# Plain outer products for the last item, splits ahead of everything else, and a GpSimd that stops computing earlier

## The chip, the cores and the metric

The kernel runs on one core of a Trainium2 chip. The metric is the device time of one execution in microseconds. TensorE (PE) does the matrix products, VectorE (DVE), ScalarE (ACT) and GpSimd (POOL) the elementwise work, and SyncE (SP) issues the DMAs.

## The reference

Attention with pooled keys and values, followed by a gated pair of matrix products, all in float32:

```
k_p, v_p = mean of k, v over 8 neighbouring positions
attn = softmax(q @ k_p.T / 8);  x = attn @ v_p       8 batches x 8 heads x 576 x 64
x -> 4608 tokens x 512
out = ((x @ w_a) * (x @ w_b)) @ w_out                512 -> 1536 -> 512
```

## The kernel before

**Precision.** Every float32 operand is split into a high part (a cast to fp32r on ACT, written with `nc.scalar.copy`) and a low part (the difference, a `tensor_tensor` subtraction, line 281, on DVE or POOL). A product is then three matmuls: high x high, high x low, low x high (lines 1352 to 1354 for inner products, 1459 to 1461 for outer ones).

**Tiling.** The tokens are taken in 6 pairs of two halves of 384 columns. The hidden width of 1536 is taken in 6 items (`j`) of two 128-row tiles. The first pair is computed with plain products. From the second pair on (`"s"` items, the ones with `p` from 1 to 5) the inner products x @ w_a and x @ w_b are done by a Strassen-like scheme with seven products in place of eight (`PRODUCTS7`). Its right operands B11, B21, T2, T1, T3, B22, T4 are made once for each pair by `prepare`: four combinations (L1099, 768 columns) and seven splits (ACT L1093, DVE or POOL L281), into the tiles `xB..` and `xT..`, of which there is one each, so that a split can run only when the pair before has used that operand for the last time. For pairs `p` from 2 on the outer products too have seven in place of eight (`OUTER7`): the gated products C11, C12, C21, C22 (the tiles `h`) are combined (L1267) and split (ACT L1259, DVE L281) into seven operands `hh` by `operands_of`, and `outer_block` does 7 products for each of 2 column parts, 42 matmuls an item, in two PSUM banks (`accX`, `accY`); after each product of three matmuls DVE adds the bank to the result `y` in SBUF (L1492), which frees it.

**Order.** The order of the work on all engines is written out by a planner in the kernel (`Machine`), which runs at build time: each piece of work has a duration, a rank (lower goes first) and conditions, and each engine takes the lowest rank that is ready. `TOP` is -1000; what empties PSUM has rank TOP or TOP + 1, gated operands TOP + 2, `prepare` a due time, the outer products 1e4 and the inner ones 2e4. The chip then executes these fixed orders with semaphores. `either` (line 271) offers a `tensor_tensor` of SBUF operands to DVE and to POOL, whichever is free first; from item number `ALONE` on, DVE alone gets it. There are 38 items: 8 of the first pair (numbers 0 to 7), then six for each of the other pairs, so number 8 is the first item of the second pair and number 14 the first of the third. In the planner, POOL's work and DVE's work of SBUF operands exclude each other. Beside the items, the attention of the next pair (`chunk`), the sums of weights for the Strassen-like products (`block_sums`) and those for the outer products (`sums_outer`, which stores its splits in DRAM as `kept_outer`) run at lower rank.

Of the kernel before, what the change touches and what calls it, by code (L numbers as in the profile page):

```python
# [9 lines left out]
F32 = mybir.dt.float32  # L10
# [73 lines left out]
SUMS_STEP = 1  # L84
SUMS_RANK = 320.0
SPARE = 1

ALONE = 14

MARGIN = 0.5  # L90

# [152 lines left out]
def attn_moe_kernel(ctx: ExitStack, tc: tile.TileContext, q, k, v, vr, wa, wb, wo, out):  # L244
# [249 lines left out]
    def sums_outer():  # L494

        for j in range(NJ):
            yield until(("kept", "raw o", 2 * j), ("kept", "raw o", 2 * j + 1))
            yield lambda: at_item[0] >= SUMS_FROM + j * SUMS_STEP and slots.can("rawo")() and len(slots.free) > SPARE
            r = slots.take("rawo", j, [P, 2, 512], F32)
            for y in range(2):  # L500
                yield transfer(r[:, y], kept["raw o", 2 * j + y], 1 << 18)
            kept["outer", j] = dr.tile([P, 2, 7, 2, P], F32, name=f"kept_outer_{j}")
            a11, a21, a12, a22 = (r[:, y, x:x + 256] for y in range(2) for x in (0, 256))

            def split(src, n, at):
                yield lambda: slots.can("osum")() and len(slots.free) >= SPARE
                e = slots.take("osum", (j, at), [P, 2, 2, 2, P], F32R)[:, :, :n]
                by = src.rearrange("p (o c s) -> p c o s", o=n, c=2)

                yield on_act(n * 256, lambda: [nc.scalar.copy(e[:, c, :, 0], by[:, c]) for c in range(2)], 2)  # L510
                yield either(n * 256, lambda eng: [low_part(eng, e[:, c, :, 1], by[:, c], e[:, c, :, 0]) for c in range(2)], 2)
                start(1e4, store(e, n, at))

            def store(e, n, at, j=j):
                for c in range(2):
                    dst = kept["outer", j][:, c, at:at + n].rearrange("p o l s -> p (o l s)")
                    yield transfer(dst, e[:, c].rearrange("p o l s -> p (o l s)").bitcast(F32), n << 17)
                mark("kept", "outer", j, at)
                slots.give("osum", (j, at))

            yield from split(r[:, 1], 2, 5)
            yield from split(a11, 1, 0)
            for out_, a, b, how in (
                (a22, a21, a22, ALU.add),
                (a21, a11, a21, ALU.subtract),
                (a11, a22, a11, ALU.subtract),
                (a12, a12, a11, ALU.subtract),
            ):
                yield either(256, lambda eng: eng.tensor_tensor(out=out_, in0=a, in1=b, op=how))
# [553 lines left out]
    def prepare(p):  # L1083
        yield lambda: have(2 * p)() and have(2 * p + 1)()
        t = xraw[p]
        b11, b12, b21, b22 = (t[:, r:r + 2, c:c + HB] for r in (0, 2) for c in (0, HB))
        rank = due_item[items.index(("s", p, 0))] - 20

        def split(name, src, *after):
            x = RIGHT.index(name)  # L1090
            yield until(("used", p - 1, x), *after)
            to = operand(p, name)
            yield on_act(2 * HB, lambda: nc.scalar.copy(to[:, 0], src))  # L1093
            yield low(2 * HB, to[:, 1], src, to[:, 0])
# [12 lines left out]
        start(rank + 2, combine(t2, b22, b11, "T2", ("T1", p)))  # L1107
        start(rank + 3, split("T2", t2, ("T2", p)))
        start(rank + 4, split("T1", b11, ("T2", p)))
        start(rank + 5, combine(b12, b22, b12, "T3", ("T1", p)))  # L1110
        start(rank + 6, split("T3", b12, ("T3", p)))
        start(rank + 7, split("B22", b22, ("T2", p), ("T3", p)))
        start(rank + 8, combine(b21, b21, t2, "T4", ("T2", p), ("operand", p, "B21")))
        start(rank + 9, split("T4", b21, ("T4", p)))
# [39 lines left out]
    def load_outer():  # L1154
        for x, name in enumerate(order_o):
            if name is None:
                continue
            j, c, second = name
            yield until(*(("kept", "outer", j, at) for at in (0, 1, 3, 5)))
            yield lambda: slots.can("wo")() and next_o[0] == x  # L1160
            next_o[0] += 1
            ops = slice(4 * second, 4 + 3 * second)
            e = slots.take("wo", x, [P, ops.stop - ops.start, 2, P], F32R)
# [79 lines left out]
    def hh_count(item):  # L1243
        if item[0] == "n":
            return 2 * len(item[1])
        return 4 if item[1] < 2 else 7

    hh_before = {item: sum(hh_count(x) for x in items[:number]) for number, item in enumerate(items)}

    def operands_of(item):  # L1250
# [150 lines left out]
    def outer():  # L1401

        x = 0
        for item in items:
            kind, p, j = item
            if kind == "s" and p >= 2:
                yield from outer_block(item, x)
                x += 4
# [6 lines left out]
            for half in halves(item):  # L1415
                yield lambda: all((item, 2 * j + y, half) in gs for y in range(2))
                for c in range(DM // P):
# [22 lines left out]
                    start(TOP + 1, taken_outer(p if kind == "s" else 0, half, c, bank, pt, opens, closes))  # L1440

    def outer_block(item, x0):
        _, p, j = item
        for c in range(2):
# [5 lines left out]
            for n, (left, right, bank, opens, what) in enumerate(OUTER7):  # L1450
# [18 lines left out]
                start(TOP + 1, taken_outer(p, half, row, bank, pt, j == 0 and first, j == NJ - 1 and last))  # L1469
            for e in ws:  # L1470
                start(TOP, give_slot(e))

    def give_operand(item, name):
        yield m.SETTLE
# [7 lines left out]
    def taken_outer(p, half, c, bank, pt, opens, closes):  # L1482
# [11 lines left out]
            mark("opened", p, half, c)  # L1494
        if p >= 2:
            yield MARGIN
        acc_free[bank] = True
# [107 lines left out]
```

## Time and profile before

| | |
|---|---|
| median of 3 runs | 1017.22 us (1015.75 to 1017.97) |
| profiled execution | 1016.27 us, span 1014.5 us |
| PE busy | 968.1 us, 95%, 5776 matmuls |
| DVE busy | 855.7 us, 84% |
| ACT busy | 579.5 us, 57% |
| POOL busy | 168.0 us, 17%, the last subtractions near 402 us |
| mean granted TensorE clock | 0.990 |

Times in the rows are microseconds from the start of the span, durations in us in the timeline and in ns where a group's mean is given. PE = matmuls of TensorE. The granted clock is given as a share of full speed. Stage by stage: the first pair ends about 226 us, the second about 398, the third begins there; the last item's inner products end near 998 us.

### The profile page before, as it was taken

To read this page: it belongs to the slowest core of one execution; us is meant where nothing else is said; L and a number is where in the kernel's file an instruction comes from. 1 tells how busy PE (TensorE), PEld (TensorE's weight loads), DVE (VectorE), ACT (ScalarE), POOL (GpSimd) and SP (SyncE) were. 2 spreads that over 40 slices of the span, in tenths; PEclk is the share of its full clock that TensorE was granted. 3 is DMA by queue.
4 is the path that set the end of the run, shared out by engine and by line. 5 is a ranking of instruction groups with operands and counts; after the bars stand their busy time and mean duration, and the time that the engine had idled before them with its cause. 6 is when DMAs were issued, how large, how long until landed. Compare 5 with 4: busy or idle time off the path is not lost.

```text
span 1014.5 us, 17014 instructions
## 1 busy us (share of the span) xinstructions
PE 968.1 (95%) x5776; PEld 953.0 (94%) x5776; DVE 855.7 (84%) x1681; ACT 579.5 (57%) x1584; POOL 168.0 (17%) x162
## 2 busy tenths in 40 slices
PE   4689999999999897999999999999999999999997
PEld 3589999999999897999999899999999999999996
DVE  7988896589897788769898988989989888968777
ACT  4789896647865565465455475455466555342331
POOL 4331233165345445000000000000000000000000
PEclk9989999999999998999999999999999999999999
DMA  9768855568876876868675696866778666796661
GB/s 311 239 229 280 283 183 191 172 206 279 302 258 237 291 278 228 302 224 313 243 272 193 221 334 222 297 234 213 268 260 311 229 224 208 258 322 239 236 208 63
DMA packets 88342, 250.16 MB, mean 247 GB/s; under 512 B 9856, under 2 KB 17536, under 8 KB 88256
## 3 DMA queue, kind: packets, MB, share of 16 engines
q1 hardware_dynamic: 88256, 249.08, 70.5%
q8 instruction: 46, 0.75, 0.3%
q14 instruction: 40, 0.33, 0.1%
HBM read 197.13 MB, written 51.90 MB: 245 GB/s over the span
## 4 chain that ended last, share of the span: by engine, by line
PE 86%; DVE 9%; ACT 2%; issue 1%; DVEq 0%; ACTq 0%
PE acc L1459 6%; PE acc L1461 6%; PE acc L1460 6%; PE psc L913 5%; PE psXB L1352 4%; PE psXB L1353 4%; PE psXB L1354 4%; PE psXA L1354 4%; PE psXA L1352 4%; PE psXA L1353 4%; PE psYA L1352 3%; PE psYA L1353 3%; PE psYA L1354 3%; PE psYB L1352 3%; PE psYB L1354 3%; PE psYB L1353 3%
## 5 line engine op out<-in xcount | busy, mean ns | idle before, releaser
L1492 DVE TENSOR_TENSOR y<-acc,y 128x384 f32<-128x384 f32 x304 | 165.0, 552 | 26.5 <-PE acc L1461 22.0
L1259 ACT CAST hh<-h 128x384 fp32r<-128x384 f32 x168 | 85.3, 516 | 92.0 <-DVE h L1397 45.5
L281 DVE TENSOR_TENSOR hh<-h,hh 128x384 fp32r<-128x384 f32 x210 | 118.1, 580 | 5.7 <-ACT hh L1306 3.3
L1459 PE MATMUL acc<-hh,wo 128*128 128x384 f32 x336 | 116.5, 347 | 1.9 <-DVE y L1492 1.2
L1460 PE MATMUL acc<-hh,wo 128*128 128x384 f32 x336 | 114.0, 339 | 2.1 <-DVE hh L281 2.0
L1461 PE MATMUL acc<-hh,wo 128*128 128x384 f32 x336 | 113.7, 338 | 0.0
L875 ACT ACTIVATE weights<-psc,least 128x72 f32<-128x72 f32 x240 | 73.8, 330 | 38.3 <-DVE least L891 34.2
L1379 ACT COPY h<-psXA 128x384 f32<-128x384 f32 x90 | 43.2, 480 | 78.2 <-PE psXA L1354 77.6
L913 PE MATMUL psc<-kdiag,qh 128*128 128x144 f32 x320 | 59.4, 286 | 11.5 <-ACT kdiag L653 10.4
L1459 PEld LDWEIGHTS acc<-hh,wo 128*128 128x128 f32 x336 | 63.5, 189 | 4.9 <-DVE y L1492 3.3
L1460 PEld LDWEIGHTS acc<-hh,wo 128*128 128x128 f32 x336 | 63.6, 189 | 2.9 <-DVE hh L281 2.9
L913 PEld LDWEIGHTS psc<-kdiag,qh 128*128 128x128 f32 x320 | 54.4, 204 | 12.4 <-issue 8.0
L1461 PEld LDWEIGHTS acc<-hh,wo 128*128 128x128 f32 x336 | 63.5, 189 | 0.0
L1267 DVE TENSOR_TENSOR h<-h,h 128x384 f32<-128x384 f32 x96 | 52.7, 549 | 0.5
L1003 ACT CAST turned<-ptr 128x512 fp32r<-128x512 f32 x72 | 40.4, 593 | 19.9 <-PE ptr L996 19.7
L875 ACT ACTIVATION_READ_ACCUMULATOR weights<-psc,least 128x1 f32 x240 | 51.6, 215 | 0.0
L818 POOL MEMSET qh<- 128x256 f32 x4 | 1.2, 311 | 296.6 <-PE psc L913 296.6
L1397 DVE TENSOR_TENSOR h<-h,h 128x384 f32<-128x384 f32 x85 | 49.5, 582 | 0.5
L1353 PE MATMUL psXA<-xT,load 128*128 128x384 f32 x144 | 48.6, 337 | 0.8 <-DVE xT L281 0.8
L1352 PE MATMUL psXA<-xT,load 128*128 128x384 f32 x144 | 48.9, 339 | 0.0
L1352 PE MATMUL psXB<-xT,load 128*128 128x384 f32 x144 | 48.5, 337 | 0.0
L1353 PE MATMUL psXB<-xT,load 128*128 128x384 f32 x144 | 48.5, 337 | 0.0
(301 smaller groups left out, 3165.4 us busy)
## 6 DMA issues: line engine op xcount, KB each, us to landing
load<-kept_S SPq DMA_DIRECT2D x96, 512.0 KB, 4.8
load<-kept SPq DMA_DIRECT2D x72, 512.0 KB, 5.1
wo<-kept_outer SPq DMA_DIRECT2D x48, 512.0 KB, 4.5
wo<-kept_outer SPq DMA_DIRECT2D x48, 384.0 KB, 3.9
kept_S<-sum SPq DMA_DIRECT2D x24, 512.0 KB, 3.2
kept_outer<-osum SPq DMA_DIRECT2D x36, 256.0 KB, 3.6
out<-y SPq DMA_DIRECT2D x48, 192.0 KB, 2.2
kept<-sum SPq DMA_DIRECT2D x18, 512.0 KB, 6.7
```

The source lines that it names most:

```text
L281: eng.tensor_tensor(out=lo, in0=src, in1=hi.bitcast(F32), op=ALU.subtract)
L875: nc.scalar.activation(s[:n, h], src[:, h - hs.start], AF.Exp, bias=least[:n, h:h + 1], scale=SCALE, accum_out=z[:n, h:h + 1],)
L913: nc.tensor.matmul(pt[:n, j * hk:(j + 1) * hk], qq[:, g, cs], kd[:, g, w].rearrange("p e s -> p (e s)"), start=(x == 0), stop=(x == len(to ...
L1259: yield on_act(HB, lambda: nc.scalar.copy(e[:, 0], gf[item, src]))
L1267: yield either(HB, lambda eng: eng.tensor_tensor(out=t, in0=ta, in1=tb, op=ALU.subtract))
L1352: nc.tensor.matmul(pt, w[:, 0, mat, c], xo[:, 0, kk], start=(opens and kk == 0), stop=False, **more)
L1353: nc.tensor.matmul(pt, w[:, 0, mat, c], xo[:, 1, kk], start=False, stop=False, **more)
L1354: nc.tensor.matmul(pt, w[:, 1, mat, c], xo[:, 0, kk], start=False, stop=(kk == 1), **more)
L1459: nc.tensor.matmul(pt, w[:, 0], e[:, 0], start=opens, stop=False, **more)
L1460: nc.tensor.matmul(pt, w[:, 0], e[:, 1], start=False, stop=False, **more)
L1461: nc.tensor.matmul(pt, w[:, 1], e[:, 0], start=False, stop=True, **more)
L1492: yield on_dve(HB, lambda: nc.vector.tensor_tensor(out=acc[at], in0=pt, in1=acc[at], op=ALU.add))
```

## The change

Three edits. (1) The last item of all does its outer products plainly: eight products (of two terms each for a row and a column half) instead of seven, on the four unmodified gated products, in six PSUM banks (the two accumulators, two banks of the inner products and the two of the attention), where the two terms of a result are added up in the bank. For this the left operand `a21` is split once more in `sums_outer` and stored, and the last item's loads hold 4 operands each. (2) The seven splits of `prepare` get the rank -999.5, just behind what empties PSUM at TOP and ahead of the adds at TOP + 1 and the gated operands at TOP + 2; the combinations keep theirs. (3) `ALONE` becomes 8 in place of 14.

```
+SPLIT_RANK = -999.5
-ALONE = 14
+ALONE = 8
...
-            kept["outer", j] = dr.tile([P, 2, 7, 2, P], F32, name=f"kept_outer_{j}")
+            kept["outer", j] = dr.tile([P, 2, 8, 2, P], F32, name=f"kept_outer_{j}")
...
             yield from split(a11, 1, 0)
+            if j == NJ - 1:
+                yield from split(a21, 1, 7)
...
-        start(rank, split("B11", b11))
+        start(SPLIT_RANK, split("B11", b11))
         start(rank, combine(b11, b12, b11, "T1", ("operand", p, "B11")))
-        start(rank + 1, split("B21", b21))
+        start(SPLIT_RANK, split("B21", b21))
...
         if kind == "s" and item[1] >= 2:
-            order_o += [(j, c, x) for c in range(2) for x in range(2)]
+            order_o += [(j, c, x, 4 if item == items[-1] else 4 - x) for c in range(2) for x in range(2)]
...
         rank = TOP + 2
+        if item == items[-1]:
+            for name, what in (("B11", "C11"), ("B22", "C22"), ("B12", "C12"), ("B21", "C21")):
+                start(rank, split(name, what, what))
+                start(rank, leave(what, "split " + name))
+            return
...
+    def outer_last(item, x0):
+        _, p, j = item
+        ws = {}
+        for c in range(2):
+            for x in range(2):
+                yield lambda: x0 + 2 * c + x in loaded_o
+                ws[c, x] = loaded_o.pop(x0 + 2 * c + x)[2]
+        banks = {}
+        a11, a12, a21, a22 = 0, 5, 7, 6
+        first = [("C11", a11), ("C21", a21)]
+        steps = [(0, *x, "B11", True, False) for x in first]
+        for c in range(2):
+            for what, l1, l2 in (("C12", a11, a12), ("C22", a21, a22)):
+                steps += [(c, what, l1, "B12", True, False), (c, what, l2, "B22", False, True)]
+        steps += [(1, *x, "B11", True, False) for x in first]
+        steps += [(c, what, left, "B21", False, True) for c in range(2) for what, left in (("C11", a12), ("C21", a22))]
+        bank_of = {"C11": ("X", "YA"), "C21": ("Y", "YB")}
+        for c, what, left, right, opens, ends in steps:
+            yield lambda: (item, right) in gq
...
+            def products():
+                nc.tensor.matmul(pt, w[:, 0], e[:, 0], start=opens, stop=False)
+                nc.tensor.matmul(pt, w[:, 0], e[:, 1], start=False, stop=False)
+                nc.tensor.matmul(pt, w[:, 1], e[:, 0], start=False, stop=ends)
+            yield on_pe(mms(3, HB), products, 1e4)
+            if ends:
+                half, row = int(what[2]) - 1, 2 * (int(what[1]) - 1) + c
+                start(TOP + 1, taken_outer(p, half, row, place, pt, False, True))
```

The rest of the diff hands `taken_outer` the bank together with the table in which it is marked free.

## Rows read from the trace of the kernel before

**Rows 1.** The page: busy time of three engines (share of the span, instructions) and the granted clock in 40 slices of 25.4 us.
```profile
PE 968.1 (95%) x5776; PEld 953.0 (94%) x5776; DVE 855.7 (84%) x1681; ACT 579.5 (57%) x1584; POOL 168.0 (17%) x162
POOL 4331233165345445000000000000000000000000
PEclk9989999999999998999999999999999999999999
```

**Rows 2.** Table of stretches: the stretch and its length, then busy us (and instructions) of PE, PEld, DVE, ACT and POOL, the granted clock, the DMA share and GB/s.
```profile
226.00:412.00 186.00, 176.01 (x1045) 172.35 (x1044) 158.81 (x286) 120.86 (x345) 87.16 (x73) 0.97 0.75 264
310.00:340.00 30.00, 26.83 (x152) 25.76 (x151) 20.96 (x39) 16.77 (x51) 14.54 (x14) 0.94 0.70 250
340.00:370.00 30.00, 29.28 (x177) 28.88 (x176) 27.64 (x53) 19.28 (x57) 15.64 (x16) 1.00 0.81 293
398.00:412.00 14.00, 10.27 (x48) 10.23 (x49) 9.67 (x13) 4.68 (x8) 3.85 (x3) 0.76 0.38 131
640.00:740.00 100.00, 100.00 (x595) 99.66 (x594) 94.04 (x196) 51.42 (x142) 0.57 (x2) 1.00 0.73 253
700.00:740.00 40.00, 40.00 (x231) 40.00 (x230) 39.39 (x79) 19.00 (x44) 0.00 (x0) 1.00 0.79 275
```

**Rows 3.** Waits of PE over 226 to 412 us: who waited for whom, us in total, times, the longest.
```profile
PE acc_s L1428 <- DVE hh L281: 5.0, 1, 5.0
PE psXB L1352 <- DVE h L1385: 1.3, 2, 0.7
PE ptr L996 <- ACT pr L970: 1.2, 1, 1.2
PE ptr L996 <- DVE rem L281: 0.9, 1, 0.9
```

**Rows 4.** Timeline at the boundary of the second and third pair: start, duration, engine, line, operation, out<-in, and in brackets the idle time before it and who ended that.
```profile
395.20 2.14 POOL L1099 TENSOR_TENSOR xraw<-xraw 128x768 f32<-128x768 f32 x1
395.58 2.57 DVE L281 TENSOR_TENSOR xT<-xraw,xT 128x768 fp32r<-128x768 f32 x1
397.29 2.52 POOL L1099 TENSOR_TENSOR xraw<-xraw,T 128x768 f32<-128x768 f32 x1
398.07 3.60 DVE L281 TENSOR_TENSOR hh<-h,hh 128x384 fp32r<-128x384 f32 x2
401.73 0.69 PE L1428 MATMUL acc_s<-hh,wo 128*128 128x384 f32 x1 [5.03 <-DVE hh L281]
```

**Rows 5.** Groups of DVE instructions over 226 to 410 us, shapes kept apart: busy us and mean ns of one, then the idle time before them.
```profile
L281 DVE TENSOR_TENSOR hh<-h,hh 128x384 fp32r<-128x384 f32 x23 | 17.5, 766 | 1.4 <-ACT hh L1306 1.0
L1397 DVE TENSOR_TENSOR h<-h,h 128x384 f32<-128x384 f32 x13 | 9.9, 765 | 0.1
L891 DVE TENSOR_SCALAR least<-m 128x4 f32<-128x4 f32 x13 | 6.1, 468 | 0.4
L281 DVE TENSOR_TENSOR xT<-xraw,xT 128x768 fp32r<-128x768 f32 x2 | 3.5, 1758 | 0.0
```

**Rows 6.** The same forms, and one of 512 columns, over 420 to 1000 us.
```profile
L281 DVE TENSOR_TENSOR hh<-h,hh 128x384 fp32r<-128x384 f32 x165 | 87.3, 549 | 1.8 <-ACT hh L1259 1.7
L1397 DVE TENSOR_TENSOR h<-h,h 128x384 f32<-128x384 f32 x71 | 39.0, 549 | 0.4
L281 DVE TENSOR_TENSOR pr<-weights,pr 128x512 fp32r<-128x512 f32 x17 | 11.6, 681 | 0.0
L281 DVE TENSOR_TENSOR xT<-xraw,xT 128x768 fp32r<-128x768 f32 x9 | 8.5, 947 | 0.0
L891 DVE TENSOR_SCALAR least<-m 128x4 f32<-128x4 f32 x32 | 5.4, 170 | 1.1
```

**Rows 7.** Timeline of the end, PE and DVE.
```profile
996.04 0.56 DVE L1397 TENSOR_TENSOR h<-h,h 128x384 f32<-128x384 f32 x1
996.30 0.34 PE L1459 MATMUL acc<-hh,wo 128*128 128x384 f32 x1
997.86 0.37 PE L1459 MATMUL acc<-hh,wo 128*128 128x384 f32 x1
999.68 0.45 PE L1460 MATMUL acc<-hh,wo 128*128 128x384 f32 x1 [1.44 <-DVE hh L281]
1010.86 0.34 PE L1461 MATMUL acc<-hh,wo 128*128 128x384 f32 x1
1011.24 0.56 DVE L1492 TENSOR_TENSOR y<-acc,y 128x384 f32<-128x384 f32 x1 [0.21 <-PE acc L1461]
```

**Rows 8.** The DMA queue of SP in the timeline of the end (the last four loads of outer weights), and two groups of DMA issues of the page (count, size of one, us to landing).
```profile
973.41 8.21 SPq L278 DMA_DIRECT2D wo<-kept_outer  x4
...
wo<-kept_outer SPq DMA_DIRECT2D x48, 512.0 KB, 4.5
out<-y SPq DMA_DIRECT2D x48, 192.0 KB, 2.2
```

**Rows 9.** The costliest group of POOL over 226 to 412 us.
```profile
L281 POOL TENSOR_TENSOR sum<-sums,sum 128x512 fp32r<-128x512 f32 x12 | 16.2, 1348 | 29.3 <-ACT sum L571 25.7 <-PE acc_s L1429 2.7 <-DMA o<-kept_ro 0.9
```

**Rows 10.** Waits of PE over 530 to 575 us, around the boundary of the third and fourth pair.
```profile
PE psXA L1353 <- DVE xT L281: 0.8, 1, 0.8
PE acc L1460 <- DVE hh L281: 0.5, 1, 0.5
```

More of the change, by code (lines that the diff above doesn't have):

```diff
@@ L1103, in prepare @@
         t2 = slots.take("T2", p, [P, 2, HB], F32)
-        start(rank, split("B11", b11))
+        start(SPLIT_RANK, split("B11", b11))
         start(rank, combine(b11, b12, b11, "T1", ("operand", p, "B11")))
-        start(rank + 1, split("B21", b21))
+        start(SPLIT_RANK, split("B21", b21))
         start(rank + 2, combine(t2, b22, b11, "T2", ("T1", p)))
-        start(rank + 3, split("T2", t2, ("T2", p)))
-        start(rank + 4, split("T1", b11, ("T2", p)))
+        start(SPLIT_RANK, split("T2", t2, ("T2", p)))
+        start(SPLIT_RANK, split("T1", b11, ("T2", p)))
         start(rank + 5, combine(b12, b22, b12, "T3", ("T1", p)))
-        start(rank + 6, split("T3", b12, ("T3", p)))
-        start(rank + 7, split("B22", b22, ("T2", p), ("T3", p)))
+        start(SPLIT_RANK, split("T3", b12, ("T3", p)))
+        start(SPLIT_RANK, split("B22", b22, ("T2", p), ("T3", p)))
         start(rank + 8, combine(b21, b21, t2, "T4", ("T2", p), ("operand", p, "B21")))
-        start(rank + 9, split("T4", b21, ("T4", p)))
+        start(SPLIT_RANK, split("T4", b21, ("T4", p)))
         yield until(("operand", p, "T2"), ("T4", p))
@@ L1157, in load_outer @@
                 continue
-            j, c, second = name
+            j, c, second, n = name
             yield until(*(("kept", "outer", j, at) for at in (0, 1, 3, 5)))
+            if second and n == 4:
+                yield until(("kept", "outer", j, 7))
             yield lambda: slots.can("wo")() and next_o[0] == x
             next_o[0] += 1
-            ops = slice(4 * second, 4 + 3 * second)
-            e = slots.take("wo", x, [P, ops.stop - ops.start, 2, P], F32R)
+            ops = slice(4 * second, 4 * second + n)
+            e = slots.take("wo", x, [P, n, 2, P], F32R)
             src = kept["outer", j][:, c, ops].rearrange("p o l s -> p (o l s)")
@@ L1245, in hh_count @@
             return 2 * len(item[1])
-        return 4 if item[1] < 2 else 7
+        return 4 if item[1] < 2 or item == items[-1] else 7
     hh_before = {item: sum(hh_count(x) for x in items[:number]) for number, item in enumerate(items)}
@@ L1405, in outer @@
             kind, p, j = item
+            if item == items[-1]:
+                yield from outer_last(item, x)
+                continue
             if kind == "s" and p >= 2:
@@ L1439, in outer @@
                         opens, closes = j == LEAD, j == LEAD - 1
-                    start(TOP + 1, taken_outer(p if kind == "s" else 0, half, c, bank, pt, opens, closes))
+                    start(TOP + 1, taken_outer(p if kind == "s" else 0, half, c, (acc_free, bank), pt, opens, closes))
     def outer_block(item, x0):
@@ L1468, in outer_block @@
                 last = what not in [t[4] for t in OUTER7[n + 1:]]
-                start(TOP + 1, taken_outer(p, half, row, bank, pt, j == 0 and first, j == NJ - 1 and last))
+                start(TOP + 1, taken_outer(p, half, row, (acc_free, bank), pt, j == 0 and first, j == NJ - 1 and last))
             for e in ws:
                 start(TOP, give_slot(e))
+    def outer_last(item, x0):
[17 more added lines that the diff above has]
+            yield lambda: (item, right) in gq
+            if opens and what in bank_of:
+                name = bank_of[what][c]
+                free = acc_free if name in acc_free else readable
+                yield lambda: free[name]
+                free[name] = False
+                tag = "acc" + name if name in acc_free else name
+                pt = ps.tile([P, HB], F32, tag=tag, name=f"acc_{p}_{j}_{c}_{what}")
+                banks[c, what] = pt, (free, name)
+            elif opens:
+                yield bank_there
+                pt, tag = take_bank(f"acc_{p}_{j}_{c}_{what}")
+                banks[c, what] = pt[:, :HB], tag
+            pt, place = banks[c, what]
+            e, w = gq[item, right][0], ws[c, left // 4][:, left % 4]
+            def products():
[6 more added lines that the diff above has]
+                start(TOP + 1, taken_outer(p, half, row, place, pt, False, True))
@@ L1496, in taken_outer @@
             yield MARGIN
-        acc_free[bank] = True
+        if isinstance(bank, str):
+            give_bank(bank)
+        else:
+            bank[0][bank[1]] = True
         if closes:
```

## The prediction

> **What bounds the kernel now.** I read the page first. TensorE is busy for 95% of the span, VectorE (DVE) for 84%, GpSimd (POOL) for 17%, and all of that POOL time lies in the first 16 of the 40 slices [rows 1]. So the time is TensorE's stream of matmuls plus the places where the stream is broken. Next I looked for those breaks with the table of stretches. Over 640 to 740 us TensorE is busy for all of 100 us although DVE is busy for 94.0 of them, and over 700 to 740 it still loses nothing with DVE at 39.4 of 40; nothing can be won there [rows 2]. In the stage of the second pair, 226 to 412 us (the only steady stage that still has POOL work), TensorE is busy for 176.0 of 186 us, and the granted clock is 0.94 over 310 to 340 and 0.76 over 398 to 412 [rows 2]. At half clock a microsecond does half the work, so the mean says what is lost: 0.06 x 30 = 1.8 us and 0.24 x 14 = 3.4 us, together 5.2. The view of waits gives the rest: the four largest waits of TensorE in that stage sum to 5.0 + 1.3 + 1.2 + 0.9 = 8.4 us [rows 3]. So the stage holds 13.6 us of breaks, and TensorE itself needs 186 - 13.6 = 172.4.
>
> The timeline shows where the 5.0 comes from. At 395.58 a DVE subtraction of 768 columns takes 2.57 us and the two of 384 columns behind it 3.60 together, while POOL runs two of its own, 2.14 and 2.52 us long; the matmul that needs the low half of `hh` is released 5.03 us late, and the half clock follows [rows 4]. The same DVE instructions are much shorter where POOL does nothing: 549 ns against 766 for `hh`, 549 against 765 for L1397, 170 against 468 for `least`, 947 against 1758 for `xT` [rows 5, 6]. Each engine here holds the other up.
>
> One more break is the end. The last matmul of the inner products is followed by 13 groups of outer products that TensorE could run in 13 x 3 x 0.173 = 6.8 us (nine matmuls lie between the starts at 996.30 and 997.86: 0.173 each). They take from 997.86 to 1011.2, that is 13.3 us: it waits 1.44 us for `hh` at 999.68, and from then on mostly for one of two accumulator banks, with the last add of DVE at 1011.24 [rows 7].
>
> **The change, part by part.**
>
> *Last item's outer products.* They grow from 42 matmuls to 48: 6 x 0.173 = 1.0 us more. Three splits (a cast on ACT and a subtraction on DVE each) and four combinations go, and eight adds into `y` stand in place of 14. What the groups wait for is now four unmodified products. C11 and C22 are made long before; C12 is made by 996.6 [rows 7] and needs one cast and one subtraction, which fit beside the last six matmuls of the inner products; C21 comes last but is needed only by the last four groups. From 996.30 on TensorE has 6 + 48 = 54 matmuls, 9.4 us, so the last starts at 996.30 + 53 x 0.173 = 1005.5, and its add follows by the same 0.38 us as before (1010.86 to 1011.24): 1005.9 against 1011.24, a gain of 5.4 us. Six banks mean that only two of the eight groups need a bank which this item used before, and an add lies at least one group behind. The stores of the last four rows (192 KB, 2.2 us to landing [rows 8]) now follow each other by about half a microsecond, for which I take off 0.4. Bounds: 5.4 if nothing is waited for; if both reused banks and the operand of C12 wait as long as the 1.44 us that the row of before shows, 5.4 - 3 x 1.44 = 1.1. I take 5.0, since every operand but one is early.
> The weights are no obstacle: the last four loads are issued between 973.41 and 981.6, and a load of 512 KB lands in 4.5 us [rows 8]; two of them grow from 384 KB. The new order asks for all four before the first group, which in the planner's time may put the first two groups behind the inner products instead of ahead of the last six; TensorE's sum is the same either way. The extra split of `a21` costs two casts, two subtractions of 128 columns and two stores on the SP queue some 600 us earlier; I price it at 0.5 us of DVE in the stage below and nothing else.
>
> *No arithmetic on GpSimd from the second pair on.* In 226 to 412 POOL is busy for 87.2 us with 73 instructions [rows 2]. A subtraction of 512 columns takes it 1348 ns [rows 9], DVE 681 [rows 6]; by that ratio the moved work is 87.2 x 681 / 1348 = 44 us on DVE. Against it stands what DVE gets back: 23 x 0.217 + 13 x 0.216 + 13 x 0.298 + 2 x 0.811 = 5.0 + 2.8 + 3.9 + 1.6 = 13.3 us, from only four forms [rows 5, 6]. DVE's need is then 158.8 + 44 - 13.3 = 189.5 us if instructions stand alone. They don't where the queue is full: 79 instructions in 39.4 us is 0.499 each [rows 2], and 286 + 73 = 359 of them make 179 us. TensorE needs 172.4. So the engine that sets this stage changes from DVE and POOL in each other's way to DVE alone, at about 179; some of the outer sums can slip into the third pair, so I take 178, a gain of 8 us of the 13.6. Bounds: 13.6 gained when DVE keeps out of the way altogether; 158.8 + 44 = 203 us when nothing of the slowing comes back, a loss of 17.
>
> Against this edit stands a rule of the Trainium skill: Perfetto Trace Analysis, section "Optimizing Scalar/DVE Operations", says that a saturated DVE may be relieved by ScalarE or even GpSimd. By it the 44 us taken back would be a loss, as in rival R2; the page adds that the two share a read port, so that it may not help, and the 3.60 us for two `hh` bear that part out.
>
> *Splits of the next pair's right operands first.* At the third boundary (around 560 us) TensorE waits 0.8 us for an `xT` subtraction and 0.5 for `hh` [rows 10]; at the fourth, inside 640 to 740, there is nothing to win [rows 2]. Each of seven splits now runs ahead of the adds and of the gated operands: behind each stand the adds on DVE, and behind those a TensorE group that wants its accumulator bank. A split of 768 columns holds them back by 0.95 us. I take 1 us gained: the `xT` wait goes and little else changes. Bounds: 1.3 gained, and 2 lost if at each of four boundaries one group then waits the 0.5 us that `hh` costs at this one.
>
> Sum: 5 + 8 + 1 = 14 us. The profiled execution took 1016.27 us (span 1014.5), so 1002.3; the median shown lies 0.95 above it, and I forecast 1003.0.
>
> **Rivals.**
> *R1, GpSimd's share is worth what it costs.* DVE, asked for 95% and more, makes TensorE wait as often as POOL did, and the stage stays at 186. For it: 340 to 370 has DVE busy for 27.6 of 30 us already; against: 700 to 740 [rows 2]. Then only 6 us are gained: 1010.5.
> *R2, DVE becomes the bound (slower).* If the long DVE instructions are long for another reason than POOL, nothing of the 13.3 comes back, DVE needs 203 us, the stage grows by 17, and the sum is 17 - 6 = 11 us slower: 1028. It decides from a need of 192 us on, where the stage's loss eats the 6 us. Against it: the same forms are short in all of 420 to 1000 [rows 6].
> *R3, every break of the stage goes.* 13.6 + 1.3 + 5.4 = 20 us: 996.5. For it: TensorE loses nothing over 100 us with DVE at 94%.
> *R4, the end doesn't get shorter.* The order written for the last item puts an add or a bank late, and the 1.0 us of added matmuls and the waits eat the gain: 1003 + 5 = 1008.
>
> **How the numbers follow.** Forecast 0.55 (997 to 1009), R1 0.18, R2 0.08, R3 0.12, R4 0.07. The range 995 to 1012.5 holds the forecast, R4, nearly all of R1 and about half of R3, some 0.85, and leaves out R2. About 2 us (0.2%) is what a measurement of this kernel can tell. Faster by more: 0.55 + 0.12 + 0.07 and most of R1, 0.87; same 0.06, the rest of R1; slower 0.07, R2.
>
> **What would show it.** After: no POOL subtraction from about 226 us on; `hh` at 550 ns in the whole stage; DVE above 95% there; no TensorE wait over 2 us near 396 and no clock under 0.9 there; the third pair's first inner products some 8 us earlier. At the end 48 matmuls without a gap over 0.5 us and some 9 us between the last inner product and the last add. The prediction fails if TensorE's waits in the second pair's stage sum to more than 14 us, with `sum` or `xT` on DVE as the releasers, or if a new half-clock stretch stands after 412 us.

## The result and the profile after

The changed kernel takes 1000.2 us (median of 4, 998.1 to 1000.8) against 1016.6 for the kernel before on the same chip: ratio 0.983, 95% interval 0.9815 to 0.9853, some 16 us gained. The profiled execution took 1000.76 us (span 999.0), clock 0.995 against 0.990.

The page of the changed kernel, the lines that answer to [rows 1] (POOL and the clock in 40 slices, now of 25.0 us):

```profile
PE 962.7 (96%) x5782; PEld 951.1 (95%) x5782; DVE 861.2 (86%) x1737; ACT 580.5 (58%) x1583; POOL 82.2 (8%) x95
POOL 4331333151000000000000000000000000000000
PEclk9989999999999999999999999999999999999999
```

GpSimd is gone from the eleventh slice on; after 226 us it has 5 instructions of 4.1 us left. DVE has 5.5 us more to do, with 56 more instructions, and its share is up by two points only.

Its table of stretches, columns as in [rows 2]:

```profile
226.00:412.00 186.00, 184.07 (x1113) 181.77 (x1112) 172.71 (x360) 123.87 (x349) 4.10 (x5) 0.99 0.78 274
310.00:340.00 30.00, 29.73 (x178) 29.02 (x177) 28.17 (x62) 18.46 (x52) 0.00 (x0) 1.00 0.72 267
340.00:370.00 30.00, 29.95 (x181) 29.55 (x180) 29.22 (x65) 19.01 (x54) 0.00 (x0) 1.00 0.78 293
398.00:412.00 14.00, 14.00 (x87) 14.00 (x86) 13.56 (x29) 7.10 (x27) 0.00 (x0) 1.00 0.67 227
640.00:740.00 100.00, 99.72 (x604) 99.14 (x603) 91.29 (x189) 52.37 (x145) 0.56 (x2) 1.00 0.73 251
```

In the same 186 us TensorE now runs 1113 matmuls in place of 1045, and DVE does 360 instructions in 172.7 us where it needed 158.8 for 286. Its busy time per instruction went from 0.555 to 0.480 us. The half clock of 310 to 340 and of 398 to 412 is gone.

TensorE's waits over 226 to 412 us of the changed kernel, which answer to [rows 3]:

```profile
PE psYA L1216 <- DVE own L282: 0.9, 1, 0.9
PE ptr L999 <- DVE rem L282: 0.6, 1, 0.6
PE psXB L1362 <- DVE h L1395: 0.3, 1, 0.3
```

They sum to 1.8 us where the four listed before made 8.4. The first two are new in place: they lie at 229 and 231 us, at the start of the stage, where the kernel before had no wait, and with them comes a stretch of half clock 3.4 us long at 231.5.

DVE forms of the changed kernel over 226 to 410 us, shapes kept apart, as [rows 5]:

```profile
L282 DVE TENSOR_TENSOR hh<-h,hh 128x384 fp32r<-128x384 f32 x27 | 14.7, 552 | 0.2
L1407 DVE TENSOR_TENSOR h<-h,h 128x384 f32<-128x384 f32 x19 | 10.5, 551 | 0.0
L282 DVE TENSOR_TENSOR xT<-xraw,xT 128x768 fp32r<-128x768 f32 x4 | 3.7, 950 | 0.0
L894 DVE TENSOR_SCALAR least<-m 128x4 f32<-128x4 f32 x13 | 2.2, 170 | 0.4
```

All four have the durations that [rows 6] show for the stages without GpSimd.

TensorE's timeline at the end of the changed kernel, which answers to [rows 7]:

```profile
986.49 0.34 PE L1364 MATMUL psXB<-xT,load 128*128 128x384 f32 x1
986.66 0.33 PE L1522 MATMUL acc_C<-hh,wo 128*128 128x384 f32 x1
...
987.71 0.34 PE L1522 MATMUL acc_C<-hh,wo 128*128 128x384 f32 x1
988.01 0.44 PE L1523 MATMUL acc_C<-hh,wo 128*128 128x384 f32 x1
...
995.10 0.34 PE L1524 MATMUL acc_C<-hh,wo 128*128 128x384 f32 x1
```

DVE's timeline of the same stretch:

```profile
987.41 1.22 DVE L282 TENSOR_TENSOR hh<-h,hh 128x384 fp32r<-128x384 f32 x2
989.19 0.56 DVE L1550 TENSOR_TENSOR y<-acc_C,y 128x384 f32<-128x384 f32 x1 [0.56 <-PE acc_C L1524]
...
993.92 2.12 DVE L1550 TENSOR_TENSOR y<-acc_C,y 128x384 f32<-128x384 f32 x4 [1.00 <-PE acc_C L1524]
```

What the kernel before lost here was not waits alone. Its table over a part of its end:

```profile
1001.30:1004.80 3.50, 3.25 (x10) 2.73 (x11) 2.71 (x6) 0.51 (x1) 0.00 (x0) 0.51 0.10 37
```

The granted clock is 0.51 there, which is 1.7 us of the 6.5 that its end took beyond unbroken matmuls; the changed kernel has no such stretch at its end. All 48 outer matmuls stand behind the last inner one, and the only break is one of 0.13 us at 988.01. The last add ends 9.6 us after the start of the last inner matmul.

**Where the time went, stage by stage.** Windows of equal time hold different work in two kernels, so I cut each trace at equal amounts of TensorE work: every matmul is counted with the time that its shape takes in an unbroken stretch at full clock (0.174 us for 384 columns), and the trace says when 150, 450, 525 and 900 us of such work had been started. The table gives the time between these marks (mark 150, mark 450 and so on); without any break the three in the middle would take about 300, 75 and 375 us. (e1 to e12 are the experiments of the next section.)

```
profiled run    to 150  150-450  450-525  525-900  900-end  span
before           191.8    317.1     79.2    376.4     50.0  1014.5
after            193.1    305.5     78.2    376.9     45.3   999.0
e1               192.1    314.5     79.3    375.9     45.2  1007.0
e2               193.6    303.9     75.5    375.7     49.5   998.2
e3               193.4    316.3     79.4    376.9     50.3  1016.3
e4               192.7    308.2     81.9    376.1     45.2  1004.1
e5               191.9    327.6     75.5    375.7     50.0  1020.7
e6               192.3    307.4     75.5    375.7     49.5  1000.4
e7               192.5    312.8     75.7    376.8     45.2  1003.0
e8               192.2    302.8     75.1    376.6     45.1   991.8
e9               192.8    303.1     75.1    376.6     46.2   993.8
e10              192.0    321.2     75.3    376.8     45.1  1010.4
e11              192.4    304.5     75.2    377.8     45.3   995.2
e12              192.8    303.8     75.1    377.9     45.2   994.8
```

Each row is one execution: the profiled one of e4 took 2.1 us more than that kernel's median and that of e10 1.6 us less, so a difference of a microsecond or two between rows can be of that kind.

Of the 15.5 us between the spans of before and after, 11.6 come from the second pair and its end (150 to 450), 4.7 from the end, 1.0 from the boundary of the third and fourth pair (450 to 525), and 1.8 are lost, most of it early.

### The profile page after: what moved, and what is told of

Read it like the earlier page. It is cut to its first block, busy times and chain, and to the rows that moved or that the text cites. A ratio compares the mean times of both kernels' runs of the same rounds, so it can differ in the third digit from the quotient of the medians.

```text
span 999.0 us, 17000 instructions
## 1 busy us (share of the span) xinstructions
PE 962.7 (96%) x5782; PEld 951.1 (95%) x5782; DVE 861.2 (86%) x1737; ACT 580.5 (58%) x1583; POOL 82.2 (8%) x95
## 4 chain that ended last, share of the span: by engine, by line
PE 90%; DVE 5%; ACT 2%; DMA 1%; issue 1%; SPq 0%; DVEq 0%; ACTq 0%
PE acc L1472 6%; PE acc L1473 5%; PE acc L1474 5%; PE psc L916 5%; PE psXB L1362 4%; PE psXB L1363 4%; PE psXB L1364 4%; PE psXA L1362 4%; PE psXA L1363 4%; PE psXA L1364 4%; PE psYA L1362 3%; PE psYA L1363 3%; PE psYA L1364 3%; PE psYB L1362 3%; PE psYB L1364 3%; PE psYB L1363 3%
## 5 line engine op out<-in xcount | busy, mean ns | idle before, releaser
L1550 DVE TENSOR_TENSOR y<-acc,y 128x384 f32<-128x384 f32 x290 | 157.5, 553 | 27.9 <-PE acc L1474 20.8
L282 DVE TENSOR_TENSOR hh<-h,hh 128x384 fp32r<-128x384 f32 x210 | 113.2, 557 | 2.9 <-ACT hh L1316 2.3
L1472 PE MATMUL acc<-hh,wo 128*128 128x384 f32 x322 | 110.7, 344 | 1.5 <-DVE y L1550 1.3
L1473 PE MATMUL acc<-hh,wo 128*128 128x384 f32 x322 | 108.6, 337 | 0.0
L1474 PE MATMUL acc<-hh,wo 128*128 128x384 f32 x322 | 108.4, 337 | 0.0
L916 PEld LDWEIGHTS psc<-kdiag,qh 128*128 128x128 f32 x320 | 54.4, 204 | 13.4 <-issue 8.5
L1472 PEld LDWEIGHTS acc<-hh,wo 128*128 128x128 f32 x322 | 60.5, 188 | 2.5 <-DVE y L1550 2.4
L1473 PEld LDWEIGHTS acc<-hh,wo 128*128 128x128 f32 x322 | 60.5, 188 | 0.4 <-DVE hh L282 0.2
L1474 PEld LDWEIGHTS acc<-hh,wo 128*128 128x128 f32 x322 | 60.4, 188 | 0.0
L1362 PE MATMUL psXB<-xT,load 128*128 128x384 f32 x144 | 48.7, 338 | 0.0
L1363 PE MATMUL psXB<-xT,load 128*128 128x384 f32 x144 | 48.4, 336 | 0.0
L1364 PE MATMUL psXB<-xT,load 128*128 128x384 f32 x144 | 48.4, 336 | 0.0
```

The source lines that it names most:

```text
L282: eng.tensor_tensor(out=lo, in0=src, in1=hi.bitcast(F32), op=ALU.subtract)
L916: nc.tensor.matmul(pt[:n, j * hk:(j + 1) * hk], qq[:, g, cs], kd[:, g, w].rearrange("p e s -> p (e s)"), start=(x == 0), stop=(x == len(to ...
L1362: nc.tensor.matmul(pt, w[:, 0, mat, c], xo[:, 0, kk], start=(opens and kk == 0), stop=False, **more)
L1363: nc.tensor.matmul(pt, w[:, 0, mat, c], xo[:, 1, kk], start=False, stop=False, **more)
L1364: nc.tensor.matmul(pt, w[:, 1, mat, c], xo[:, 0, kk], start=False, stop=(kk == 1), **more)
L1472: nc.tensor.matmul(pt, w[:, 0], e[:, 0], start=opens, stop=False, **more)
```

## The experiments

**One edit each, and one left out.** e1 has the six banks and plain products alone (`ALONE = 14`, splits at their old ranks), e2 has `ALONE = 8` alone, e3 the first-rank splits alone, e4 all but the splits:

```
e2, against before
-ALONE = 14
+ALONE = 8
...
e4, against after (all seven splits)
-        start(SPLIT_RANK, split("B11", b11))
+        start(rank, split("B11", b11))
```

e1: 

> The kernel before with the last item's plain outer products alone. Theory A (the three edits add up: the end gives 5 us, GpSimd's withdrawal 8 to 10, the splits 1): about 1011 us, 5 under before, with no difference ahead of 960 us but the few hundred nanoseconds of the extra split. Theory B (the end is short only because the whole item arrives in another order after the other two edits): no more than 2 us under before, 1014 or more.

e2: 

> The kernel before with ALONE = 8 alone: no arithmetic on GpSimd from the second pair on. Theory A: 1006 to 1008 us, the 5 us wait near 396 and both half-clock stretches of the second pair's stage gone. Theory C (what broke the stage was the order of the next pair's operands, and the rank of the splits mended it): the stall at the boundary stays in some form, and no more than 3 us are gained, 1013 or more.

e3: 

> The kernel before with the rank of the seven splits alone. Theory A: between 1015 and 1018, within 1.5 us of before, and the long DVE instructions beside GpSimd stay where they are. Theory C: 6 us or more under before, 1010 or less, with the wait at the boundary of the second and third pair gone though GpSimd still works there.

e4: 

> The changed kernel without the rank of the splits (the end and ALONE = 8 stay). Theory A: 1001 to 1003, 1 to 2 us over the changed kernel's 1000.2. Theory C: 1008 or more. If the rank costs something at the start of the second pair (the changed kernel has a new half-clock stretch of 3.4 us at 231 us, and its first Strassen-like product starts 5.6 us later than before), this kernel is faster than the changed one: 997 to 999.

Measured, in us and as ratio to before with its 95% interval: e1 1009.1 us, 0.9930 [0.9918, 0.9942]; e2 999.1, 0.9826 [0.9812, 0.9839]; e3 1017.3, 1.0004 [0.9995, 1.0013]; e4 1003.8, 0.9878 [0.9865, 0.9892]. The edits don't add up: in ratio, -0.7% and -1.7% for e1 and e2 make -2.4%, their combination e4 gives only -1.2%, and `ALONE = 8` alone is as fast as all three edits together. Against what was expected: e3 came out as theory A had it, and e4 0.8 us above A's range. e1 gained 7.3 us where A had 5; 2.6 of them lie between marks 150 and 450, where the expectation had no difference. e2 gained 17 us where A had 8 to 10. Theory C falls with e2 and e3.

The table says where the edits fail to add up. The end takes 45.1 to 45.3 us wherever the last item is plain in six banks and 49.5 to 50.3 where it isn't; in the three pairs that differ in little else there (before and e1, e2 and e4, e3 and after) that is 4.8, 4.3 and 5.0 us, and this part does add up. What doesn't is the boundary after mark 450, 75.5 us in e2 and 81.9 in e4, and the second pair, 303.9 and 308.2. The table of stretches over 540 to 575 us of e2, where the view of TensorE's waits lists none:

```profile
540.00:575.00 35.00, 35.00 (x210) 34.88 (x209) 34.32 (x73) 17.90 (x55) 0.00 (x0) 1.00 0.75 250
```

The same stretch of e4:

```profile
540.00:575.00 35.00, 32.06 (x178) 30.42 (x177) 31.42 (x58) 17.25 (x44) 0.00 (x0) 0.90 0.56 182
```

And TensorE's waits there, in e4:

```profile
PE acc L1472 <- DVE y L1550: 2.4, 2, 1.6
PE psXA L1363 <- DVE xT L282: 0.6, 1, 0.6
```

In e2 the fourth pair's attention rows (the last ACT copy into `xraw` before `prepare`) are there at 520.8 us, in e4 at 542.8, in the changed kernel at 542.5 and before at 551.4. `prepare` has 11 DVE instructions of 768 columns to do behind them, and at 550 us TensorE wants their results. That made the theory for e7 and e8.

**Is it GpSimd's reading that costs?** e5 and e6 take e2's kernel and let GpSimd work beside DVE in items 8 to 13 on a tile that nobody reads, so that DVE's own list of work stays as it is; e6 is the control whose added work beside the 64-column subtraction writes only:

```
+        nc.gpsimd.tensor_tensor(out=idle[:, 1, :64], in0=part.bitcast(F32), in1=idle[:, 0, :64], op=ALU.subtract)
e5
+        for _ in range(3):
+            nc.gpsimd.tensor_tensor(out=idle[:, 1], in0=idle[:, 0], in1=idle[:, 0], op=ALU.subtract)
e6
+        for _ in range(6):
+            nc.gpsimd.memset(idle[:, 1], 0.0)
```

e5: 

> The kernel with ALONE = 8 alone (999.1 us), with GpSimd kept busy beside VectorE in items 8 to 13 by work that nobody reads: after each 384- or 512-column remainder that VectorE makes there, GpSimd subtracts 64 of its columns and then three times 96 columns from a tile of its own. No instruction of the other engines is changed. Theory A (GpSimd's arithmetic costs VectorE its port, so its withdrawal pays because the rest of VectorE's work runs shorter): hh of 384 columns goes from some 550 ns to 620 to 770 in the stage, and 4 to 12 us come back: 1003 to 1011. Theory B (the gain is from shorter chains and a better order alone): hh stays within 30 ns and the time within 2 us: 998 to 1001.

e6: 

> The same, but the three subtractions from its own tile are six memsets of 96 columns: GpSimd is about as busy, and reads nothing. Control for the waits that the dependent 64-column subtraction brings. Theory A as a matter of two-input reads: hh within 40 ns of 550 and the time within 2 us of 999.1. If memsets hold up VectorE as well, hh is as long as beside the subtractions and so is the time. Theory B: 998 to 1001 for both.

Measured: e5 1022.7 us, 1.0070 [1.0055, 1.0085], 23.6 above e2; e6 1002.4, 0.9864 [0.9848, 0.9879], 3.2 above e2. Two groups of DVE over 226 to 410 us in e2:

```profile
L282 DVE TENSOR_TENSOR hh<-h,hh 128x384 fp32r<-128x384 f32 x26 | 14.3, 551 | 0.4
L1405 DVE TENSOR_TENSOR h<-h,h 128x384 f32<-128x384 f32 x19 | 10.5, 552 | 0.0
```

The same two in e5:

```profile
L282 DVE TENSOR_TENSOR hh<-h,hh 128x384 fp32r<-128x384 f32 x23 | 14.4, 625 | 3.8 <-ACT hh L1327 3.8
L1418 DVE TENSOR_TENSOR h<-h,h 128x384 f32<-128x384 f32 x18 | 11.9, 663 | 0.0
```

The largest group of GpSimd in e5, over 226 to 412 us:

```profile
L290 POOL TENSOR_TENSOR idle<-idle 128x96 f32<-128x96 f32 x232 | 116.3, 501 | 18.2
```

The two groups of DVE in e6:

```profile
L282 DVE TENSOR_TENSOR hh<-h,hh 128x384 fp32r<-128x384 f32 x25 | 14.0, 560 | 0.3 <-ACT hh L1327 0.2
L1418 DVE TENSOR_TENSOR h<-h,h 128x384 f32<-128x384 f32 x19 | 11.2, 590 | 0.0
```

And the largest group of GpSimd in e6:

```profile
L290 POOL MEMSET idle<- 128x96 f32 x474 | 84.5, 178 | 27.4
```

Both times lie outside the expected ranges: e5 far above theory A's 1003 to 1011, with `hh` inside its 620 to 770 ns, and e6 1.2 us above A's 2 us, with `hh` inside A's 40 ns; theory B falls. Work of GpSimd that takes nothing over from DVE costs 20.3 us more when most of it reads two operands than when most of it only writes. All of it lies between marks 150 and 450 (327.6 against 307.4), and the rest of the table agrees to 0.5 us. One confound remains: GpSimd is busy for 155.0 us of 226 to 412 in e5 and for 127.9 in e6, and ACT waits for the dummy work to let go of a tile for 13.4 us in e5 and 10.7 in e6, so a part of the 20 may be that GpSimd is fuller. How large that part can be, the tables of stretches between the marks 150 and 450 say, of e2, e5 and e6 in this order:

```profile
193.60:497.50 303.90, 302.02 (x1842) 299.45 (x1841) 275.40 (x565) 190.78 (x539) 19.96 (x17) 1.00 0.78 271
191.90:519.50 327.60, 308.90 (x1841) 302.65 (x1840) 292.56 (x565) 190.17 (x539) 174.72 (x333) 0.98 0.72 252
192.30:499.70 307.40, 302.74 (x1841) 299.30 (x1840) 278.74 (x565) 190.17 (x539) 145.02 (x570) 1.00 0.76 268
```

DVE runs 565 instructions in all three and is busy for 17.2 us longer in e5 than in e2, in e6 for 3.3. So 13.9 us of the 20 between e5 and e6 appear as DVE's own stretching. The granted clock is 0.98 in e5 and 1.00 in e6; at half clock for 10.2 us in all (from 352 and from 403 us), e5 loses some 5 us more. That leaves little for a fuller GpSimd, but since DVE is not busy all the time in e5, it is not shown that each of the 13.9 us reaches TensorE.

Which instructions stretch shows in the kernel before. Its groups of DVE over 226 to 395 us:

```profile
L1492 DVE TENSOR_TENSOR y<-acc_s,y 128x384 f32<-128x384 f32 x32 | 17.6, 554 | 7.7 <-PE acc_s L1429 7.5
L681 DVE TENSOR_REDUCE kv<-kraw 128x72 f32<-128x576 f32 x7 | 5.1, 741 | 0.0
```

The add of a PSUM bank to a tile, 554 ns, and the reduction of one tile, 741, are as long beside GpSimd as without it (551 and 744 after 420 us); the subtractions of two SBUF tiles grow from 549 to 766 and `least`, a TENSOR_SCALAR, from 170 to 468 (means over 226 to 410 us) [rows 5, 6]. Such a mean mixes two kinds. In the trace of the kernel before, between 226 and 410 us, 15 of the 23 `hh` subtractions overlap no instruction of GpSimd and take 552 ns on the mean; the 8 that overlap one take 1167, the longest 2150. Of the 36 adds of `acc_s`, 25 overlap one and take 554 ns, and so do the other 11. The Trainium skill, SBUF — State Buffer, section "Who interferes with whom", says which do: DVE instructions with two SBUF inputs meet GpSimd's reads at a shared port, and so do those in a two-port mode, where reductions and instructions with one SBUF input do not. These runs agree for the two-input subtractions, the adds from PSUM and the reductions, with the numbers above; that `least` runs in a two-port mode no run here shows.

**The boundary after mark 450.** e7 is the changed kernel with the attention's chunks released one item earlier, e8 the same without the split rank:

```
-            x = lo + (hi - lo) * (i % (2 * PER_HALF)) // (2 * PER_HALF) - 1
+            x = lo + (hi - lo) * (i % (2 * PER_HALF)) // (2 * PER_HALF) - 2
```

e7: 

> The changed kernel (1000.2 us) with one edit: the attention's chunks are released one item earlier in all pairs. At the boundary before the fourth pair (548 to 560 us) the changed kernel loses 2 us, the kernel with ALONE = 8 alone none; there the fourth pair's attention rows are ready at 521 us, in the changed kernel at 542. Theory A (what is lost at the boundary is set by how early these rows are ready): rows ready at 525 or earlier, the loss gone, 998.0 to 998.8. Theory B (the loss comes from the splits of the right operands, which are first in the order): the rows are earlier and the time is the same, 999.5 to 1001. It gets slower, over 1002, if the earlier chunks take VectorE from the products of the items before.

e8: 

> The last item's six banks and ALONE = 8, the splits at their old ranks (1003.8 us so far: it lost some 6.5 us at the boundaries at 404 and 560 us that the kernel with ALONE = 8 alone did not lose), with the chunks released one item earlier. Theory A (readiness of the attention rows): the boundary costs nothing, as in the kernel with ALONE = 8 alone, and with the shorter end the sum is 999.1 - 4.8 = 994 to 996. Theory B (the order of the splits decides): 1002 to 1005, as without the edit.

Measured: e7 1004.5 us, 0.9887 [0.9871, 0.9904]; e8 993.5 us, 0.9782 [0.9768, 0.9797]. At the boundary both do what theory A says: the rows are ready at 506.8 and 515.2 us and the boundary costs 75.7 and 75.1, nothing. The other runs of the table say the same. In before, after, e1, e3 and e4 the rows come 42 to 44 us behind mark 450, and the stretch to mark 525 takes 78.2 to 81.9 us; in the nine others they come 1 to 23 us behind it, and it takes 75.1 to 75.7. Why e2 has them 20 us earlier than e4, which differs by the last item alone, is not shown. e8 also beats both kernels, by 23 us and by 7, and comes out half a microsecond under A's 994 to 996. e7 as a whole missed its expectation: it loses 7.3 us to the changed kernel in the second pair. The stretch 376 to 396 us in e7's table:

```profile
376.00:396.00 20.00, 14.74 (x72) 13.45 (x72) 18.43 (x37) 10.49 (x30) 0.00 (x0) 0.89 0.75 253
```

The two longest of the waits there, in e7's timeline of TensorE:

```profile
380.48 0.44 PE L1440 MATMUL acc_s<-hh,wo 128*128 128x384 f32 x1 [1.50 <-DVE y L1550]
...
389.21 0.44 PE L1362 MATMUL psXA<-xT,sum 128*128 128x384 f32 x1 [1.97 <-ACT sum L574]
```

The same stretch in e8's table:

```profile
376.00:396.00 20.00, 19.82 (x114) 19.50 (x113) 19.77 (x38) 11.32 (x22) 0.00 (x0) 1.00 0.87 307
```

DVE does as many instructions in both, 37 and 38; in e7 they are in an order in which TensorE waits. The split rank alone separates these two kernels: between marks 150 and 450 it costs 10.0 us here and gains 2.7 between e4 and after (less than that if e4's 2.1 us, named under the table, lie there); the 0.8 between before and e3 is no more than executions of one kernel differ by.

**Three parts of e8 by themselves, and one step further.** e9 gives the last item two banks, e10 sets `ALONE = 14`, e11 `ALONE = 0`, e12 releases the chunks one item earlier still:

```
e9
-        steps += [(1, *x, "B11", True, False) for x in first]
-        steps += [(c, what, left, "B21", False, True) for c in range(2) for what, left in (("C11", a12), ("C21", a22))]
-        bank_of = {"C11": ("X", "YA"), "C21": ("Y", "YB")}
+        for c in range(2):
+            for (what, left), l2 in zip(first, (a12, a22)):
+                steps += [(c, what, left, "B11", True, False), (c, what, l2, "B21", False, True)]
+        bank_of = {"C11": ("X", "X"), "C21": ("Y", "Y"), "C12": ("X", "X"), "C22": ("Y", "Y")}
```

e9: 

> The kernel of e8 (993.5 us; six plain banks at the end, ALONE = 8, chunks earlier, splits at their old ranks) with the last item's plain products in two banks only: each result's pair of rounds runs through bank X or Y, C12 and C22 first, and all of B11's and B21's rounds last. Theory A (the end gains from the plain order, since no combination of right operands stands ahead of it; the banks count little, because a bank is read by one addition of some 0.55 us while the other is filled by 6 matmuls of 1.0 us): 993.5 to 994.8. Theory B (the six banks are what shortens it, since additions stand between two uses of a bank): gaps of 0.5 us and more in front of several of the 8 uses, 995.5 to 999.

e10: 

> The kernel of e8 (993.5 us) with ALONE = 14 as before: GpSimd shares VectorE's arithmetic in items 8 to 13 again. Theory A (the sharing itself costs some 11 us between 226 and 412 us, wherever the boundaries fall): 1002 to 1007, hh at some 760 ns and half-clock stretches near 340 to 400. Theory B (the loss in that stretch came from late attention rows, which the earlier release mends without touching GpSimd): 993 to 997.

e11: 

> The kernel of e8 (993.5 us) with ALONE = 0: GpSimd makes no sum or remainder in the first 226 us either, where it is busy for 39 us of the first 116 and 39 of the next 110. Theory A (sharing pays nowhere): TensorE has no wait from 116 to 226, so nothing is to be gained there; in the first 116 us, where VectorE is 83% busy and TensorE 77%, 1 to 4 us are gained: 989.5 to 992.5. Theory B (it pays where VectorE alone would not keep up): the start has its 39 us of GpSimd's instructions, some 20 us of VectorE's own time, and loses 3 to 12 us: 996.5 to 1005.

e12: 

> The kernel of e8 (993.5 us) with the attention's chunks released two items earlier than in the changed kernel instead of one. Theory A (early attention rows mend the boundaries, and beyond that VectorE has about as much to do as fits beside TensorE): e8 loses nothing over 0.35 us at any one place after 116 us, so nothing more is to be had: 992.5 to 996. Theory B (each such edit re-deals the breaks, and e8 without one was a lucky deal): breaks of 2 us and more come back at 244, 390 or 560 us, 997 to 1006.

Measured: e9 994.7 us, 0.9790 [0.9777, 0.9804]; e10 1013.9, 0.9972 [0.9962, 0.9983]; e11 996.0, 0.9801 [0.9787, 0.9814]; e12 996.3, 0.9805 [0.9792, 0.9819].

e9: as theory A had it. The end is 1.1 us longer than in e8. The timeline of TensorE in e9 has one wait there, for an operand and not for a bank:

```profile
981.75 0.45 PE L1524 MATMUL acc_C<-hh,wo 128*128 128x384 f32 x1 [0.76 <-DVE hh L282]
```

So the plain products make the gain at the end, 46.2 us against 49.5 to 50.3, and the six banks are worth at most the 1.1. Since e9 changes the order of the rounds together with the banks, what its one wait comes from is not separated; the row names an operand.

e10: the arithmetic on GpSimd costs 20 us here, more than theory A's 9 to 14, and `hh` takes 905 ns on the mean where A had some 760; theory B falls. Between marks 150 and 450 it takes 18.4 us more than e8. Where it breaks most shows in the timelines. GpSimd's in e10:

```profile
399.21 4.08 POOL L282 TENSOR_TENSOR xT<-xraw,xT 128x768 fp32r<-128x768 f32 x2
```

DVE's in e10:

```profile
399.60 3.98 DVE L282 TENSOR_TENSOR osum<-rawo,osum 128x256 fp32r<-128x256 f32 x2
403.50 2.62 DVE L282 TENSOR_TENSOR hh<-h,hh 128x384 fp32r<-128x384 f32 x2
```

TensorE's in e10:

```profile
406.17 0.69 PE L1441 MATMUL acc_s<-hh,wo 128*128 128x384 f32 x1 [5.45 <-DVE hh L282]
```

It is the picture of [rows 4] again, at the same boundary: two subtractions of 256 columns, 0.75 us together when GpSimd is still, take 3.98 beside two of GpSimd's, `hh` comes behind them, and the matmul waits 5.45 us.

e11: neither theory's number. Without GpSimd's arithmetic the first pair loses nothing (TensorE is busy for all of 110.0 us from 116 to 226, with DVE at 90.1), and to mark 150 it takes 192.4 us against 192.2. What e11 loses to e8, 2.5 us between the medians and 3.4 between the profiled spans, lies later: 1.7 in the second pair and 1.2 between 525 and 900. So sharing neither pays nor costs in the first pair.

e12: no break over 0.9 us came back after 100 us, and the boundary stays at 75.1; the 2.8 us above e8 are spread: 0.6 before mark 150, 1.0 in the second pair, 1.3 between 525 and 900. That is just above theory A's range and below B's: the early rows mend the boundary in general, and the last 2 or 3 us of e8 depend on the order.

## Why the prediction was right, step by step

**Forecast.** 1003.0 us against 1000.2, inside the forecast's 997 to 1009 and the wider 995 to 1012.5: the second pair's stage and the end are where the time came from. The sum of the steps, 5 + 8 + 1, was met by other terms: 4.7 at the end, 11.6 in the second pair, 1.0 at a boundary that the splits were to mend, and 1.8 lost. That the total came out within 1.5 us of the sum is in part luck: one step was too small by 3.6, and the 1.8 us were lost where no step had a term.

**The last item's outer products** (5.0 taken, bounds 1.1 to 5.4). Right in size and in its working: 4.3 to 5.0 us in the pairs of runs, 48 matmuls, no gap over 0.13 us, some 9 us from the last inner product to the last add. The planner put all eight groups behind the inner products, as the step allowed. What the step said of six banks was nearly beside the point (e9, 1.1 us). Its reading of the end before, that TensorE waits mostly for banks, left out the stretch at a clock of 0.51; the gain was right all the same, since the new end was priced at the unbroken rate.

**No arithmetic on GpSimd** (8 taken). The sign and the mechanism were right: `hh` at 552 ns, no wait near 396, no half clock there. GpSimd too was held up, as the prediction had it: its combinations of 768 columns at 395 and 397 us take 2.14 and 2.52 us [rows 4], one at 204.8 us beside no such work of DVE 1.82. The mis-sized term is DVE's need, "359 of them make 179 us" at 0.499 us each, a pace borrowed from 700 to 740 us, where the mix is another. The stage of the kernel before held 1045 matmuls; the changed kernel runs about as many from 226 us on in 11.6 us less:

```profile
226.00:400.40 174.40, 172.47 (x1042) 170.17 (x1041) 161.55 (x335) 117.63 (x325) 4.10 (x5) 0.99 0.78 276
```

DVE needs 161.6 us there, with 335 instructions at 0.482 each; 24 fewer than the step's 359, which the order puts outside the stage. What it got back was undercounted as well: over all forms, its instructions of 226 to 412 us before are together some 20 us longer than the same operations and shapes take in after, e2 and e8, where the step had 13.3 from four forms. So DVE does not set the stage at 179; it ends beside TensorE, whose breaks go almost wholly, as in rival R3. The prediction that DVE would stand "above 95%" failed for the same reason: 172.7 of 186 is 93%. The lower bound, 17 us lost when nothing of the slowing comes back, fell: in the four forms that it counted all of it came back. How much the sharing costs depends on the rest: 17 us by itself (e2), 13.2 of them between marks 150 and 450, and 20 between e10 and e8, 18.4 of them there; the step took 13.6 us of breaks for the most that could be won.

**Splits first** (1 taken, bounds 1.3 gained to 2 lost). Wrong in part, and the size rests on luck. The edit by itself does nothing (e3): the boundary that it was to mend takes 79.4 us in e3 and 79.2 before. Between e4 and the changed kernel it did there what the step said: the `xT` wait goes, and TensorE waits for the adds instead, 1.3 us in place of 2.4; the boundary takes 78.2 us in place of 81.9. The changed kernel's waits over 540 to 575 us:

```profile
PE acc L1472 <- DVE y L1550: 1.3, 2, 1.0
```

What mends the boundary wholly is that the attention rows are ready early (e7, e8, e12 and e2), and then it is worth 4.1 us (79.2 before, 75.1 in e8), not the 1.3 of the two waits that the step summed. In the second pair, for which the step had no term, the edit costs 10.0 us between e8 and e7 and gains 2.7 between e4 and after, beyond both bounds; why it goes one way or the other is open. What the step missed besides is the new break at 228 to 231 us: it stands in the two kernels that have the split rank and no earlier chunks (after and e3), and not in e2 and e4.

**Rivals.** R1, a stage that stays at 186, fell: the breaks go. R4 fell: the end is 4.8 us shorter. R3, 996.5, came nearest in its mechanism for the second pair; the changed kernel misses it by the new break of the split rank and by the boundary after mark 450, and e8, which has neither, took 993.5. R2 fell, with its condition.

## What to carry to other kernels

In this kernel GpSimd's share of the arithmetic was worth nothing in the first pair (e11) and cost 17 to 20 us behind it, where it slowed DVE. Before counting work that is moved to a second elementwise engine as relief, compare the same form of instruction with and without it beside, apart by where the operands lie and by whether the two overlap. Where an engine is full, an edit of order has no price of its own: try each edit alone and without each, cut the traces at equal work, and look for the one input that comes late (here the attention rows) before moving what waits for it. At the end of a kernel, fewer matmuls can cost more than plain ones if they need combinations first (here 42 against 48, and 4.3 to 5.0 us).

## What was not expected

Memsets of GpSimd, with the 64-column subtractions beside them, stretched DVE's two-input instructions little (`hh` 560 ns against 551, the products `h` 590 against 552) although GpSimd was busy for 127.9 of 186 us; with two-input subtractions in their place they took 625 and 663. And a DVE with nothing to spare need not make TensorE wait: over 545 to 565 us of e8 DVE is busy for 19.72 of 20 us and TensorE for 20.00.
